# Moving GpSimd's mask work, the first token blocks and w_out's column sums in a fused window attention and feed-forward kernel

## The chip, the cores and the metric

The kernel runs on one core of a Trainium2 chip. The metric is the device time of one execution in microseconds (us); lower is better. TensorE (PE) multiplies matrices, VectorE (DVE) and ScalarE (ACT) work element by element, GpSimd (POOL) does the same and makes masks, and SyncE (SP) issues every DMA here. Each engine runs its own queue in order; semaphores tie the queues together.

## The reference

q, k and v have 8 sequences, 8 heads, 576 tokens and 64 channels. Each token attends to the 32 tokens on either side of it; the heads are then laid side by side and go through a feed-forward layer.

```python
scores = 1/sqrt(64) * q @ k.T                    # per head
mask = abs(pos[:, None] - pos[None, :]) <= 32
attn = softmax(where(mask, scores, -1e9))
x = (attn @ v)                                   # 4608 tokens x 512
h = x @ w_in                                     # 512 x 2048
g = s * relu(h)**2 + b
out = g @ w_out                                  # 2048 x 512
```

All inputs and the output are float32.

## The kernel before

The kernel multiplies in bfloat16, so q, k, v, w_in and w_out are loaded as float32 and cast on the chip. `b` is not added to g: since every g gets the same b, the kernel adds b times the column sums of w_out to the output. These sums, times b, are the tile CVEC.

Nothing in the program is in an order written by hand. Every piece of work is given to `_Graph.add` with an engine (stream), reads, writes, a key and an estimated cost. `plan` simulates the engines with these costs and picks, at each moment, the job that can start first, the key breaking ties; `emit` then writes the queues with the semaphore waits. A key is thus a wish and not a place, and a changed size or an estimated latency (`HELD`, which delays in the plan what uses a piece of w_out) moves other work in the queues. What shares a buffer keeps the order of the calls to `add`.

The stages that matter here, all in the first 70 us:

- **Sequence 0** (`load_pair`, `turn_pair`, `pair_scores`, `first_units`). q and k are loaded by pairs of heads, cast (L687), transposed on TensorE (L700), copied out of PSUM (L705, L706), and multiplied to scores (L939) whose mask is already in PSUM: `opened` adds the tile NEG (L957). GpSimd makes IDENT and NEG first of all (`band`, two selects each, L482 and L487). The five units of `first_units` multiply by v (L864), normalise (L888, L890), and are transposed (L897) and copied to XT (L905).
- **Weights** (`load_weights`). Eight pieces of w_in and eight of w_out, 512 KB each, go through a ring of eight staging tiles STG; GpSimd casts all sixteen (L553). Every load is queued on SP, the w_out loads each waiting for a staging tile.
- **Three early blocks** (`s1`, `early`). The first 512 tokens are split in blocks of 96, 256 and 160 tokens, `sizes`. `s1` multiplies a block by 128-column slices of w_in into one of two PSUM banks W (L1119), 4 or 2 slices to a bank by the block's size (`group`); ScalarE takes the relu into one of three tiles R1 (L1126), and VectorE squares it into GT (L1128). The list `FIRST` gives the order of calls, (block, quarter of w_in), with TURN where the next pair of heads of sequence 1 is put in between, since its transposes use the same banks W. `early` multiplies GT by w_out into four accumulators of 128 tokens each, two in O and two in AVN (L1168); VectorE scales them and adds CVEC (L1153).
- **Masks** (`masks`). From sequence 1 on scores are masked after the exponential by the tiles MASKS. GpSimd makes them after `first_units`: four selects, three copies (L517), four small memsets (L520).
- **Column sums** (`colsum`). TensorE sums w_out's columns into bank SC (L1182, 64 small matmuls), VectorE copies the four parts into a block diagonal of a spare output tile (L1186), one float32 matmul spreads them over the partitions (L1189), and VectorE multiplies by b (L1191). GpSimd clears the two spare tiles first (L1180, L1181).
- **Sequence 1** is turned as sequence 0 was, k cast by VectorE and q by GpSimd (L687). Its scores use SC.
- **Later sequences** are transposed by DMA, and the main loop alternates w_in (L1119) and w_out (L1137) for blocks of 256 and 512 tokens.

Of the kernel before, what the change touches and what calls it, by code (L numbers as in the profile page):

```python
# [9 lines left out]
ALU = mybir.AluOpType  # L10
# [9 lines left out]
NUNIT = (NTILE + 1) // 2  # L20
# [12 lines left out]
TURN = (None, 0)  # L33
FIRST = ((0, 0), (1, 0), (0, 1), (1, 1), (2, 0), (2, 1), (0, 2), (1, 2), (2, 2), TURN, (0, 3), TURN, (1, 3), TURN, (2, 3), TURN)
WOUTE = (("pool", "pool"),) * 4
TAIL = ("act", "dve")
HOST = (("k", 3), ("q", 0))
HELD = (2200.0, 1500.0, 1000.0, 1000.0)
OPEN = -24.4
# [287 lines left out]
def bass_sliding_window_symmetric__then__act_starrelu_kernel(  # L327
# [12 lines left out]

    sizes = [96, 256, 160, 256, 256]
    NE = 3
# [8 lines left out]
    with ExitStack() as es:  # L351
# [18 lines left out]

        NSTG, NNAT, NEX, NXN, NR1, NOUT, XR = 8, 6, 5, 5, 3, 5, 2048
        WIN_BF = sb((128, 4, DFF), BF16, "win")
# [16 lines left out]
        MASK = MASKS[0]  # L389
# [32 lines left out]
        add = g.add  # L422
# [71 lines left out]
        for p0 in (0, 64):  # L494
            band(NEG[p0:p0 + 64, :], NEG[p0:p0 + 64, :], ("NEG", p0), 0, 64, -97, -FAR, source=("NEG", p0))
        ones = ONESW.rearrange("p (one c) -> p one c", one=1).to_broadcast((128, 4, 128))
        add("pe", [lambda e: e.matmul(W[:, 1, :].rearrange("p (a c) -> p a c", a=4), lhsT=ONESW[:, :], rhs=ones,
# [86 lines left out]
        def cast_v(c, u, key, eng, slack):  # L584
            vs, vb, n = number(c, u) % NUNIT, number(c, u) % (2 * NUNIT), 64 * len(tiles(c, u))
            add(eng, (lambda e: e.copy(VB[0:n, vb, :, 0:D], VST[0:n, vs, :, :])) if eng == "act" else
                (lambda e: e.tensor_copy(VB[0:n, vb, :, 0:D], VST[0:n, vs, :, :])),  # L587
                {"act": 617.0, "dve": 420.0, "pool": 750.0}[eng],
                reads=[("VST", vs)], writes=[("V", vb, y) for y in (0, 1)], key=key, slack=slack)

        def load_rows(y, load_key):
# [427 lines left out]
        def attention():  # L1019
            seq = {"k": -200.0}  # L1020

            def nxt():
                seq["k"] += 1.0
                return seq["k"]
# [31 lines left out]
            for step in ORDER1:  # L1056
# [119 lines left out]
        def colsum():  # L1176

            even, block = OUTS[NOUT - 2][:, 0:128], OUTS[NOUT - 1][:, :]
            made = [land["av", 0, NUNIT - 1]]
            add("pool", lambda e: e.memset(even, 1.0 / 32), 150, writes=[("OUTS", NOUT - 2)], key=-19.0, waits=made)  # L1180
            add("pool", lambda e: e.memset(block, 0.0), 500, writes=[("OUTS", NOUT - 1)], key=-19.0, waits=made)  # L1181
            add("pe", [lambda e, fc=fc, x=x: e.matmul(  # L1182
                SC[32 * x:32 * x + 32, 0, 0:128], lhsT=ONESW[:, 0:32], rhs=WOUT_BF[:, fc, 128 * x:128 * x + 128],
                start=(fc == 0), stop=(fc == 15)) for fc in range(16) for x in range(4)],
                1100, reads=["ONESW"] + [("Wout", i, x) for i in range(4) for x in (0, 1)], writes=[("SC", 0)], key=-12.0)
            add("dve", [lambda e, x=x: e.tensor_copy(block[32 * x:32 * x + 32, 128 * x:128 * x + 128],  # L1186
                                                     SC[32 * x:32 * x + 32, 0, 0:128]) for x in range(4)],
                800, reads=[("SC", 0)], writes=[("OUTS", NOUT - 1)], key=-12.0)
            add("pe", lambda e: e.matmul(SC[:, 1, :], lhsT=even, rhs=block, start=True, stop=True),  # L1189
                950, reads=[("OUTS", NOUT - 2), ("OUTS", NOUT - 1)], writes=[("SC", 1)], key=-12.0)  # L1190
            add("dve", lambda e: e.tensor_scalar(CVEC[:, :], SC[:, 1, :], SB128[:, 1:2], None, ALU.mult),  # L1191
                680, reads=[("SC", 1), ("SB128", 1)], writes=[("CVEC", x) for x in (0, 1)], key=P2[0])

# [280 lines left out]
```

## Time and profile before

| | us |
|---|---|
| median of 3 runs | 316.41 |
| lowest and highest run | 315.55, 317.66 |
| the profiled execution, its whole time | 318.05 |
| the profiled execution, its span in the profile | 316.3 |

| engine | busy us | share of the span |
|---|---|---|
| PE | 303.9 | 96% |
| DVE | 194.8 | 62% |
| ACT | 141.9 | 45% |
| POOL | 91.7 | 29% |

The profile is of one execution. A line of a timeline gives start and length in us, engine, source line, operation, what it writes and reads, the tile's size, how many instructions are merged (x8), and in brackets the idle time of the engine before it and what ended that. PE's lengths contain some 0.17 us in which a matmul drains while the next runs, so the time of a group is read from its start to the next group's start. The granted clock is the share of TensorE's full clock.

### The profile page before, as it was taken

The page shows a single profiled execution, that of the slowest core. Times are in us where ns is not written, and L with a number is a line of the kernel's source. Part 1 is how long each engine was busy: PE and PEld are TensorE (multiplying, and loading weights), DVE is VectorE, ACT ScalarE, POOL GpSimd, SP SyncE. Part 2 cuts the span into 40 slices and gives each one's busy share as a digit, 9 for nine tenths or more (in the row PEclk, how much of TensorE's full clock was granted, in tenths as well). Part 3 has the DMA queues.
Part 4 walks back from the last instruction along what each step waited for, and adds up shares of the span by engine and source line. Part 5 has one row for each costly group of instructions (what it writes and reads, how often), then busy time and mean ns, then how long its engine had stood idle before and what let it go on. Part 6 is the DMA issues. An engine that isn't in the chain of part 4 may idle for free.

```text
span 316.3 us, 7961 instructions
## 1 busy us (share of the span) xinstructions
PE 303.9 (96%) x3348; PEld 161.6 (51%) x3348; DVE 194.8 (62%) x387; ACT 141.9 (45%) x224; POOL 91.7 (29%) x110
## 2 busy tenths in 40 slices
PE   6888969999999999999999999999999999999995
PEld 2466656567664454544444444444444444444444
DVE  4666465895897897795577576967445543333312
ACT  4746326356544775654265435444444333333300
POOL 3468973670406136131513411451000000000000
PEclk9799979999999999999999999999999999999999
DMA  6999999998994998799799799996221110000022
GB/s 214 330 380 388 360 229 241 225 188 296 248 182 137 297 166 164 242 206 153 184 290 151 149 251 313 167 169 157 64 63 51 52 46 33 35 35 33 36 96 74
DMA packets 100055, 56.10 MB, mean 177 GB/s; under 512 B 72048, under 2 KB 91248, under 8 KB 100016
## 3 DMA queue, kind: packets, MB, share of 16 engines
q1 hardware_dynamic: 100016, 55.56, 73.0%
q8 instruction: 27, 0.44, 0.6%
q14 instruction: 12, 0.10, 0.1%
HBM read 36.70 MB, written 9.44 MB: 146 GB/s over the span
## 4 chain that ended last, share of the span: by engine, by line
PE 83%; DMA 5%; POOL 4%; SPq 3%; DVE 3%; issue 1%; POOLq 0%
PE w L1119 36%; PE o L1137 35%; PE avn L864 4%; DMA stg<-in_moe_w_in_dram 4%; POOL wout L553 3%; PE sc L806 2%; DMA stg<-in_v_dram 1%; PE avn L1168 1%; SPq L662 1%; PE o L1168 1%; DVE outs L1153 1%; PE w L700 1%; PE avn L897 1%; SPq L673 1%; DVE vb L587 1%
## 5 line engine op out<-in xcount | busy, mean ns | idle before, releaser
L1119 PE MATMUL w<-xt,win 128*128 128x512 bf16 (+3 forms) x768 | 144.8, 327 | 1.1 <-issue 0.6
L1126 ACT ACTIVATE r<-w 128x512 bf16<-128x512 f32 (+2 forms) x148 | 86.6, 586 | 104.0 <-PE w L1119 87.6
L1137 PE MATMUL o<-wout,gt 128*128 128x512 bf16 (+1 forms) x528 | 126.8, 373 | 0.3 <-DVE gt L1128 0.3
L1128 DVE TENSOR_TENSOR gt<-r 128x512 bf16<-128x512 bf16 (+2 forms) x148 | 77.2, 526 | 75.9 <-ACT r L1126 75.5
L1119 PEld LDWEIGHTS w<-xt,win 128*128 128x128 bf16 x768 | 67.7, 98 | 53.9 <-issue 0.8
L1137 PEld LDWEIGHTS o<-wout,gt 128*128 128x128 bf16 x528 | 50.7, 98 | 55.8 <-DVE gt L1128 0.6
L755 POOL CAST nat<-stg 128x1024 bf16<-128x1024 f32 (+1 forms) x21 | 26.6, 1265 | 64.4 <-DMA stg<-in_q_dram 42.5
L772 POOL COPY kt<-ktr 128x512 bf16<-128x512 bf16 (+1 forms) x30 | 31.1, 1037 | 37.4 <-DMA ktr<-nat 35.9
L834 ACT ACTIVATE ex<-sc 128x1024 bf16<-128x1024 f32 (+1 forms) x28 | 28.6, 1023 | 22.5 <-PE avn L864 21.7
L1153 DVE SCALAR_TENSOR_TENSOR outs<-o,sb,cvec 128x512 f32<-128x512 f32 (+1 forms) x35 | 25.4, 728 | 11.4 <-PE o L1137 11.3
L890 DVE TENSOR_TENSOR xn<-avn,rec 128x512 bf16<-128x512 f32 (+1 forms) x31 | 21.3, 688 | 1.0 <-DVE rec L888 0.2
L838 DVE TENSOR_TENSOR ex<-ex,mask 128x1024 bf16<-128x1024 bf16 (+1 forms) x28 | 21.2, 757 | 1.1 <-ACT ex L834 0.5
L864 PE MATMUL avn<-vb,ex 64*64 64x65 bf16 x944 | 19.9, 197 | 0.3
L864 PEld LDWEIGHTS avn<-vb,ex 64*64 64x64 bf16 x944 | 12.9, 106 | 13.2 <-issue 7.8
L755 DVE CAST nat<-stg 128x1024 bf16<-128x1024 f32 (+1 forms) x15 | 12.2, 810 | 3.7 <-DMA stg<-in_k_dram 1.9
L587 DVE CAST vb<-vst 128x512 bf16<-128x512 f32 (+1 forms) x28 | 13.8, 494 | 0.8 <-DMA vst<-in_v_dram 0.7
L888 DVE RECIPROCAL rec<-avn 128x8 f32<-128x8 f32 (+1 forms) x31 | 6.2, 201 | 8.3 <-PE avn L864 8.0
L806 PE MATMUL sc<-qt,kt 64*64 64x128 bf16 x432 | 11.3, 216 | 0.0
L700 PE MATMUL w<-ident,nat 128*128 128x128 bf16 x64 | 7.0, 253 | 3.9 <-POOL nat L687 3.4
L905 ACT COPY xt<-avn 128x512 bf16<-128x512 bf16 (+2 forms) x14 | 7.1, 516 | 6.3 <-PE avn L897 6.3
L705 ACT COPY qt<-w 128x512 bf16<-128x512 bf16 x8 | 4.7, 584 | 11.3 <-PE w L700 11.3
L553 POOL CAST win<-stg 128x1024 bf16<-128x1024 f32 x8 | 8.6, 1080 | 3.6 <-DMA stg<-in_moe_w_in_dram 3.4
(119 smaller groups left out, 156.8 us busy)
## 6 DMA issues: line engine op xcount, KB each, us to landing
out_dram<-outs SPq DMA_DIRECT2D x35, 256.0 KB, 2.6
vst<-in_v_dram SPq DMA_DIRECT2D x28, 256.0 KB, 4.4
stg<-in_k_dram SPq DMA_DIRECT2D x6, 1024.0 KB, 10.6
stg<-in_q_dram SPq DMA_DIRECT2D x6, 1024.0 KB, 6.4
stg<-in_moe_w_in_dram SPq DMA_DIRECT2D x8, 512.0 KB, 9.3
stg<-in_moe_w_out_dram SPq DMA_DIRECT2D x8, 512.0 KB, 10.3
stg<-in_q_dram SPq DMA_DIRECT2D x8, 256.0 KB, 5.3
stg<-in_k_dram SPq DMA_DIRECT2D x8, 256.0 KB, 5.1
```

Source lines behind the costliest of these rows:

```text
L553: add(eng, (lambda e: e.copy(dst, stg)) if eng == "act" else (lambda e: e.tensor_copy(dst, stg)), {"act": 1040.0, "dve": 690.0, "pool": 11 ...
L755: add(eng, lambda e, x=x: e.tensor_copy(nat[0:top, 1024 * x:1024 * x + 1024].rearrange("p (i h d) -> p h i d", h=H, i=2), stg[0:top, :].re ...
L772: add("pool", lambda e, c=c, w=w: e.tensor_copy(KT[slot][:, :, c:c + w].rearrange("p a (s i) -> p a s i", i=4), KTR[slot][:, :, :, c // 4: ...
L834: add("act", lambda e, dst=flat_dst, src=flat_src: e.activation(dst, src, AF.Exp, bias=0.0, scale=0.125), 190 + 0.833 * 512 * len(hs), rea ...
L838: add("dve", lambda e, flat=flat, mask=mask: e.tensor_tensor(flat, flat, mask, ALU.mult), 130 + 0.53 * 512 * len(hs), reads=[("E", ei, hp, ...
L864: return [lambda e: e.matmul(av[64 * x:64 * x + 64, h, 0:D + 1], lhsT=buf[64 * g:64 * g + 64, h % 2, h // 2, c:c + 64], rhs=VB[64 * g:64 * ...
L890: add("dve", lambda e: e.tensor_tensor(XN[xi][0:p1, :].rearrange("p (a c) -> p a c", a=H), av[0:p1, :, 0:D], REC[ri][0:p1, :].rearrange("p ...
L1119: add("pe", [lambda e, g=g, kc=kc: e.matmul(wt[:, g, :], lhsT=WIN_BF[:, kc, (f0 + g) * 128:(f0 + g + 1) * 128], rhs=XT[:, kc, t0 % XR:t0 % ...
L1126: add("act", lambda e: e.activation(rt, wt, AF.Relu, bias=0.0, scale=1.0), 190 + 0.833 * ng * nt, reads=[("W", wb)], writes=[("R1", rb)], ...
L1128: add("dve", lambda e: e.tensor_tensor(GT[gs][:, f0:f0 + ng, g0:g0 + nt], rt, rt, ALU.mult), 130 + 0.53 * ng * nt, reads=[("R1", rb)], wri ...
L1137: add("pe", [lambda e, fc=fc: e.matmul(O[:, ob, 0:cn], lhsT=GT[gs][:, fc, g0:g0 + 128], rhs=WOUT_BF[:, fc, c0:c0 + cn], start=(fc == 0), s ...
L1153: add("dve", lambda e: e.scalar_tensor_tensor(OUTS[us][:, 0:cn], bank, SB128[:, 0:1], CVEC[:, c0:c0 + cn], ALU.mult, ALU.add), 200 + 1.07 ...
```

## The change

GpSimd makes the base mask and clears the two spare tiles right after NEG, ahead of its first cast; the copies and cuts of the mask wait for the last v cast of sequence 1. The first three blocks are 224, 128 and 160 tokens. FIRST has another order of blocks and turns, two entries of HELD go from 1000 to 1500, R1 has four tiles instead of three, and the column sums use bank 1 of AVN, which is also the fourth accumulator of `early`, instead of SC.

```diff
-FIRST = ((0, 0), (1, 0), (0, 1), (1, 1), (2, 0), (2, 1), (0, 2), (1, 2), (2, 2), TURN, (0, 3), TURN, (1, 3), TURN, (2, 3), TURN)
+FIRST = ((0, 0), (0, 1), (1, 0), (1, 1), (2, 0), (0, 2), (2, 1), (1, 2), (2, 2), (0, 3), TURN, TURN, (1, 3), TURN, (2, 3), TURN)
-HELD = (2200.0, 1500.0, 1000.0, 1000.0)
+HELD = (2200.0, 1500.0, 1500.0, 1500.0)
-    sizes = [96, 256, 160, 256, 256]
+    sizes = [224, 128, 160, 256, 256]
-        NSTG, NNAT, NEX, NXN, NR1, NOUT, XR = 8, 6, 5, 5, 3, 5, 2048
+        NSTG, NNAT, NEX, NXN, NR1, NOUT, XR = 8, 6, 5, 5, 4, 5, 2048
...
+        for p0 in (0, 64):
+            band(MASK[p0:p0 + 64, :], ONESW[p0:p0 + 64, :], ("MASK", 0, p0), 0, 64, -96)
+        even, block = OUTS[NOUT - 2][:, 0:128], OUTS[NOUT - 1][:, :]
+        done = [g.tasks[-1]]
+        add("pool", lambda e: e.memset(even, 1.0 / 32), 150, writes=[("OUTS", NOUT - 2)], key=-95.0, waits=done)
+        add("pool", lambda e: e.memset(block, 0.0), 500, writes=[("OUTS", NOUT - 1)], key=-95.0, waits=done)
...
         def masks(after):
-            for p0 in (0, 64):
-                band(MASK[p0:p0 + 64, :], ONESW[p0:p0 + 64, :], ("MASK", 0, p0), 0, 64, -24.0, waits=[after])
             for i, cuts in ((1, ((0, 96), (64, 0))), (2, ((64, 96),)), (3, ((0, 0),))):
                 add("pool", lambda e, i=i: e.tensor_copy(MASKS[i][:, :], MASK[:, :]), 250,
-                    reads=[("MASK", 0, 0), ("MASK", 0, 64)], writes=[("MASK", i, 0), ("MASK", i, 64)], key=0.0)
+                    reads=[("MASK", 0, 0), ("MASK", 0, 64)], writes=[("MASK", i, 0), ("MASK", i, 64)], key=0.0, waits=[after])
...
-            masks(land["av", 0, NUNIT - 1])
...
+            masks(land["vb", 1])
...
         def colsum():
-            made = [land["av", 0, NUNIT - 1]]
-            add("pool", lambda e: e.memset(even, 1.0 / 32), 150, writes=[("OUTS", NOUT - 2)], key=-19.0, waits=made)
-            add("pool", lambda e: e.memset(block, 0.0), 500, writes=[("OUTS", NOUT - 1)], key=-19.0, waits=made)
             add("pe", [lambda e, fc=fc, x=x: e.matmul(
-                SC[32 * x:32 * x + 32, 0, 0:128], lhsT=ONESW[:, 0:32], ...
+                AVN[32 * x:32 * x + 32, 1, 0:128], lhsT=ONESW[:, 0:32], ...
...
-            add("pe", lambda e: e.matmul(SC[:, 1, :], lhsT=even, rhs=block, start=True, stop=True),
+            add("pe", lambda e: e.matmul(AVN[:, 1, :], lhsT=even, rhs=block, start=True, stop=True),
...
-            add("dve", lambda e: e.tensor_scalar(CVEC[:, :], SC[:, 1, :], SB128[:, 1:2], None, ALU.mult),
+            add("dve", lambda e: e.tensor_scalar(CVEC[:, :], AVN[:, 1, :], SB128[:, 1:2], None, ALU.mult),
```

TensorE's queue in the new program, from the first w_out matmul to the fourth accumulator's first (columns x count; "k0" are the transposes of k of pair 0, "acc3" is the third accumulator): acc1 x2, w_in 224 x8, acc2 x2, 160 x8, acc3 x2, 160 x8, acc1 x2, 128 x16, 160 x8, acc2 x2, acc3 x2, 160 x8, 224 x8, acc1 x2, 224 x8, acc2 x2, k0 x4, column sums x64, q0 x4, acc3 x2, k1 x4, acc1 and acc2 x4, q1 x4, L1189, 128 x16, transposes x4, scores of pair 0, acc4 x4. VectorE's queue in the same place: k0's cast, a square, k1's cast, k0's copy out of PSUM, a square, the four copies of the column sums.

More of the change, by code (lines that the diff above doesn't have):

```diff
@@ L589, in cast_v @@
                 reads=[("VST", vs)], writes=[("V", vb, y) for y in (0, 1)], key=key, slack=slack)
+            land["vb", c] = g.tasks[-1]
         def load_rows(y, load_key):
@@ L1176, in colsum @@
         def colsum():
-            even, block = OUTS[NOUT - 2][:, 0:128], OUTS[NOUT - 1][:, :]
-            made = [land["av", 0, NUNIT - 1]]
-            add("pool", lambda e: e.memset(even, 1.0 / 32), 150, writes=[("OUTS", NOUT - 2)], key=-19.0, waits=made)
-            add("pool", lambda e: e.memset(block, 0.0), 500, writes=[("OUTS", NOUT - 1)], key=-19.0, waits=made)
             add("pe", [lambda e, fc=fc, x=x: e.matmul(
-                SC[32 * x:32 * x + 32, 0, 0:128], lhsT=ONESW[:, 0:32], rhs=WOUT_BF[:, fc, 128 * x:128 * x + 128],
+                AVN[32 * x:32 * x + 32, 1, 0:128], lhsT=ONESW[:, 0:32], rhs=WOUT_BF[:, fc, 128 * x:128 * x + 128],
                 start=(fc == 0), stop=(fc == 15)) for fc in range(16) for x in range(4)],
-                1100, reads=["ONESW"] + [("Wout", i, x) for i in range(4) for x in (0, 1)], writes=[("SC", 0)], key=-12.0)
+                1100, reads=["ONESW"] + [("Wout", i, x) for i in range(4) for x in (0, 1)], writes=[("AVN", 1)], key=-12.0)
             add("dve", [lambda e, x=x: e.tensor_copy(block[32 * x:32 * x + 32, 128 * x:128 * x + 128],
[L1187 to L1192, printed above, removed]
+                                                     AVN[32 * x:32 * x + 32, 1, 0:128]) for x in range(4)],
+                800, reads=[("AVN", 1)], writes=[("OUTS", NOUT - 1)], key=-12.0)
+            add("pe", lambda e: e.matmul(AVN[:, 1, :], lhsT=even, rhs=block, start=True, stop=True),
+                950, reads=[("OUTS", NOUT - 2), ("OUTS", NOUT - 1)], writes=[("AVN", 1)], key=-12.0)
+            add("dve", lambda e: e.tensor_scalar(CVEC[:, :], AVN[:, 1, :], SB128[:, 1:2], None, ALU.mult),
+                680, reads=[("AVN", 1), ("SB128", 1)], writes=[("CVEC", x) for x in (0, 1)], key=P2[0])
         units, made = attention(), 0
```

## The prediction

> **What bounds the kernel now.** I read the page first (busy shares, then the 40 slices), next the busy time by stretches, then TensorE's own timeline where it was not full.
>
> ```profile
> PE 303.9 (96%) x3348; PEld 161.6 (51%) x3348; DVE 194.8 (62%) x387; ACT 141.9 (45%) x224; POOL 91.7 (29%) x110
> ```
> ```profile
> 40.00:50.00 10.00, 8.01 (x121) 6.21 (x122) 6.97 (x13) 2.54 (x5) 6.67 (x13) 0.83 1.07 228
> 50.00:60.00 10.00, 10.00 (x136) 5.69 (x133) 6.58 (x12) 6.85 (x11) 3.80 (x6) 1.00 1.18 261
> ```
>
> The columns are the stretch, its length, busy PE, PEld, DVE, ACT, POOL, granted clock, DMA share and GB/s. TensorE is the bound and is full from 50 us on; what can be won lies earlier, above all at 40 us, where both busy time and clock dip. TensorE's timeline (start, length, group, idle before it):
>
> ```profile
> 30.98 0.61 PE L1168 MATMUL o<-wout,gt 128*128 128x512 bf16 x2 [0.74 <-POOL wout L553]
> ...
> 32.41 1.72 PE L1119 MATMUL w<-xt,win 128*128 128x96 bf16 x24
> 33.97 0.59 PE L1168 MATMUL avn<-wout,gt 128*128 128x512 bf16 x2
> ...
> 36.69 0.72 PE L1119 MATMUL w<-xt,win 128*128 128x160 bf16 x8
> 37.24 0.59 PE L1168 MATMUL o<-wout,gt 128*128 128x512 bf16 x2
> 37.67 1.03 PE L1168 MATMUL avn<-wout,gt 128*128 128x512 bf16 x4
> ...
> 41.99 0.99 PE L700 MATMUL w<-ident,nat 128*128 128x128 bf16 x8 [2.42 <-POOL nat L687]
> 42.90 1.90 PE L1182 MATMUL sc<-wout,onesw 128*32 128x128 bf16 x64
> ...
> 46.85 1.04 PE L1119 MATMUL w<-xt,win 128*128 128x256 bf16 x8
> 47.73 0.39 PE L700 MATMUL w<-ident,nat 128*128 128x128 bf16 x4
> 47.95 1.08 PE L1189 MATMUL sc<-outs 128*128 128x512 f32 x2
> ```
>
> TensorE runs dry at 39.57 (41.99 - 2.42) and stands 2.42 us until the first transposes of sequence 1, which wait for GpSimd's cast of q. The stall costs a second time: the clock is granted in stretches of 3.41 us (one at half speed begins at 7.94, one at 42.07), and each follows a poorly filled one:
>
> ```profile
> 4.53:7.94 3.41, 1.97 (x30) 1.02 (x29) 1.34 (x3) 1.69 (x3) 0.61 (x1) 1.00 0.97 294
> 7.94:11.36 3.42, 3.04 (x29) 1.70 (x30) 2.05 (x4) 1.20 (x3) 1.23 (x2) 0.50 1.09 367
> 28.42:31.83 3.41, 2.54 (x30) 1.91 (x29) 2.40 (x5) 1.76 (x4) 3.14 (x5) 1.00 1.05 383
> 31.83:35.24 3.41, 3.41 (x41) 2.77 (x39) 1.13 (x3) 1.52 (x3) 3.16 (x5) 1.00 1.05 386
> 38.66:42.07 3.41, 0.99 (x7) 0.28 (x5) 1.25 (x1) 0.00 (x0) 3.13 (x5) 1.00 0.80 244
> 42.07:45.49 3.42, 3.42 (x81) 3.03 (x82) 1.95 (x5) 0.70 (x2) 2.30 (x6) 0.50 0.97 230
> ```
>
> Stretches 58% (1.97 of 3.41) and 29% busy were followed by half clock, one 74% busy was not. So the stall loses 2.42 us, and half of 3.42, 1.71 us, after it.
>
> **What the stall waits for.** GpSimd's timeline, and two DMA issues asked for one at a time (the last piece of w_out, and k of pair 0 of sequence 1):
>
> ```profile
> 2.79 0.29 POOL L482 TENSOR_SCALAR_AFFINE_SELECT neg<-neg 64x128 bf16<-64x128 bf16 x1
> 3.22 0.29 POOL L487 TENSOR_SCALAR_AFFINE_SELECT neg<-neg 64x128 bf16<-64x128 bf16 x1
> 6.76 0.61 POOL L687 CAST nat<-stg 128x512 bf16<-128x512 f32 x1 [3.25 <-DMA stg<-in_q_dram]
> ...
> 28.13 1.26 POOL L553 CAST win<-stg 128x1024 bf16<-128x1024 f32 x1 [0.32 <-DMA stg<-in_moe_w_in_dram]
> ...
> 33.93 0.52 POOL L1181 MEMSET outs<- 128x512 f32 x1
> ...
> 40.14 1.04 POOL L553 CAST wout<-stg 128x1024 bf16<-128x1024 f32 x1
> 41.24 0.68 POOL L687 CAST nat<-stg 128x512 bf16<-128x512 f32 x1
> ...
> 50.68 1.44 POOL L587 CAST vb<-vst 128x512 bf16<-128x512 f32 x2 [0.77 <-DMA vst<-in_v_dram]
> 55.13 1.04 POOL L755 CAST nat<-stg 128x1024 bf16<-128x1024 f32 x1 [3.01 <-DMA stg<-in_k_dram]
> ```
> ```profile
> L550 SPq DMA_DIRECT2D stg<-in_moe_w_out_dram x1: 367/367/367, 29.4 to 29.4; - x1
> ...
> DMA to landing us min/median/max: 9.4/9.4/9.4
> ```
> ```profile
> L662 SPq DMA_DIRECT2D stg<-in_k_dram x1: 368/368/368, 32.4 to 32.4; - x1
> ...
> DMA to landing us min/median/max: 7.8/7.8/7.8
> ```
>
> From 29.39 (28.13 + 1.26) GpSimd never waits; its last w_out cast ends at 41.18. Between casts stand mask selects, copies and memsets. But w_out's last piece lands only at 38.8 (29.4 + 9.4), the eight pieces 1.36 us apart (524 kB each at the 386 GB/s of the stretch from 31.83), so the first about 29.3; k of sequence 1 lands at 40.2 (32.4 + 7.8).
>
> **The change, part by part.**
>
> *Masks and memsets ahead of the first cast.* Eight casts of 1.04 us with 0.065 between them (40.14 + 1.04 to 41.24) would end at 29.39 + 8.84 = 38.2. The data do not allow it: the last piece lands at 38.8, so the last cast ends at 38.85 + 1.04 = 39.9, 1.3 us earlier and not 3. The first ends near 30.5 instead of 30.93, since no select precedes it, so w_out's first matmuls move up by up to 0.44.
> Ahead of the first cast GpSimd now has four more selects of 0.43 from start to start (2.79 to 3.22) and memsets of 128 and 512 elements, at the cast's rate (1.04 for 1024) 0.65 with two gaps 0.78: 3.51 + 1.72 + 0.78 = 6.0, and the cast waits for its DMA until 6.76: cover 0.75, cost 0. Without that cover, every 0.1 us over delays three q casts by 0.1. The select that TensorE's -FAR matmuls need moves one select back, 0.43; a TensorE wait in that stage, for the cast that starts at 6.76, takes it up.
> The seven mask copies and cuts now follow the last v cast (ends at 50.68 + 1.44 = 52.1): about 1.8 us (estimate: seven small jobs of half a select to a select), to 54, before the cast at 55.13, which waited 3.01 us. Cost 0; if k landed early, at most 1.8 on a cast that does not set the end.
>
> *The restart.* In the new order TensorE's first transposes after its dry point are k's, so VectorE's cast decides, not GpSimd's q cast.
>
> ```profile
> 34.80 1.04 DVE L1128 TENSOR_TENSOR gt<-r 128x512 bf16<-128x512 bf16 x1 [0.62 <-ACT r L1126]
> ...
> 40.21 1.25 DVE L687 CAST nat<-stg 128x512 bf16<-128x512 f32 x1 [1.76 <-DMA stg<-in_k_dram]
> 43.01 0.69 DVE L706 COPY kt<-w 128x512 bf16<-128x512 bf16 x1 [1.55 <-PE w L700]
> ...
> 44.85 1.19 DVE L1186 COPY outs<-sc 32x128 f32<-32x128 f32 x4 [0.51 <-PE sc L1182]
> 46.07 0.44 DVE L687 CAST nat<-stg 128x512 bf16<-128x512 f32 x1
> ...
> 49.09 0.74 DVE L1191 TENSOR_SCALAR cvec<-sc,sb 128x512 f32<-128x512 f32 x1
> ```
>
> The same cast took 1.25 us while GpSimd was casting and 0.44 when it was not. From 40.21 that gives a restart between 40.7 and 41.5. GpSimd's q cast now runs at about 40.0 to 40.6, over half of that: I take 41.05, 0.94 earlier than 41.99 (0.47 to 1.28).
>
> *Blocks, turns, HELD.* Blocks of 224, 128, 160 have the columns of 96, 256, 160 (512) and as many matmuls: total work 0. What moves is the share ahead of the dry point. Before, 16 matmuls each of 96, 256 and 160 columns came after it. Eight of 256 take 0.88 (46.85 to 47.73), eight of 160 take 0.55 (36.69 to 37.24), 16 of 96 take 1.56 - 0.88 = 0.68 (32.41 to 33.97): 3.54 us. Now 16 of 128 (0.055 each, from 47.73 to 47.95) and 16 of 160 come after: 1.98. So 1.56 us of w_in work moves ahead; of w_out's matmuls 16 instead of 20 stand there, four fewer, 0.86 (two take 0.43, 37.24 to 37.67). Net 0.7 us less is left after the restart (0.4 to 0.7). TensorE would run dry near 39.6, as before (its start is up to 0.44 earlier, 0.2 of the moved work falls into the 0.74 idle before 30.98), and stand about 1.4 us.
>
> *The clock.* 1.4 us idle is 59% busy if one stretch holds all of it, next to the 58% that lost the clock; cut by an edge, it lies nearer the 74% that kept it. I count half of 1.71: 0.85 (0 to 1.71).
>
> *Four relu tiles.* They remove ScalarE's waits for VectorE's squares; from 24 to 44 us these are (total, times, longest):
>
> ```profile
> ACT r L1126 <- DVE gt L1128: 0.4, 1, 0.4
> ```
>
> ScalarE is 45% busy; worth 0 (to 0.3).
>
> *Column sums in the fourth accumulator.* SC is freed for the scores, but the fourth accumulator's 16 matmuls must all follow L1189 and the CVEC product. Between the column sums and L1189 TensorE now has 12 transposes (0.66) and six w_out matmuls (1.30): 1.95 us. VectorE must do the k cast of pair 1, one kt copy (0.69), a square and the four copies (1.19) first. With k's transposes and the sums (half of 1.90 at full clock) done near 42.2 TensorE asks at 44.1, and the copies end near 44.4: a wait of 0.3 (0 to 1.2). Behind it stand w_in, transposes and pair 0's scores, for which ScalarE's exp waits. The CVEC product (0.74) then hides behind 16 matmuls of 128, four transposes and the scores.
>
> Sum: -0.94 - 0.7 - 0.85 + 0.3 = -2.2. SP's order is the same through this stage: no DMA term. The profiled execution took 318.05 (span 316.3, 1.75 around it) and would take 315.9; it stood 1.64 above the median of the runs, 316.41, from which the same step gives 314.2. Best of each bound: -1.28 - 0.7 - 1.71 = -3.7, 312.7.
>
> **The rivals.**
> 1. *The clock is kept as well:* an edge of the 3.41 us stretches cuts the remaining idle time, so that none is as empty as 58%: -0.94 - 0.7 - 1.71 + 0.3 = -3.05, 313.4, and 312.7 with the other bounds. For it: 1.4 us is shorter than the 2.42 that lost the clock. Against it: all 1.4 in one stretch leaves 59%, next to the losing row. The Trainium skill, TensorE: Matmul & The Clock Gate, Part 1, also would keep the clock here, since there half speed returns after about 3.4 us of idling; the trace disagrees with that figure, since 2.42 us of idling was enough.
> 2. *The stall only moves:* restart at 41.5, half clock kept, 0.7 at L1189: -0.47 - 0.7 + 0.7 = -0.5, 315.9. For it: the DMA times, which the change does not touch.
> 3. *Slower: the fourth accumulator.* TensorE's queue is in order, and VectorE reaches the four copies behind k0's cast, a square, k1's cast, a kt copy and a second square. At the longest prices above, 41.46 + 1.04 + 1.25 + 0.69 + 1.04 + 1.19 = 46.7. TensorE, restarted at 41.5, asks at 44.6; 2.1 us idle brings a second half clock, 1.71. With the first kept: +2.1 + 1.71 - 0.47 - 0.7 = +2.6, 319.0. It decides once the copies end over 1.4 us after TensorE asks. Against it: GpSimd has gaps there, and one square, not both, need be late.
>
> **How the numbers follow.** Forecast 0.43 (own range 313.0 to 315.6), rival 1 0.30, rival 2 0.17, rival 3 0.10. A measurement can tell about 1%, 3.2 us. Faster by over 1% (under 313.25): over half of rival 1, since the runs scatter by 0.9 below their median (315.55), and a quarter of the forecast, 0.29; slower by over 1% (above 319.57): a part of rival 3 and what I have not seen, 0.08; within: 0.63. Range 311.8 to 317.4: rival 1's best less that 0.9, up to the middle between rivals 2 and 3.
>
> **What would show it.** Right: GpSimd casting only from 29.4, waiting about 0.3 us for DMA before each w_out cast, the last ending near 39.9; TensorE idle 1.0 to 1.8 us instead of 2.42, ended by VectorE's k cast at 40.7 to 41.5; at most one half-clock stretch there; L1189 entered by a wait for VectorE under 0.7; the w_in work of 256 columns earlier by about the sum. Wrong: w_out landing earlier than before, a wait over 1.2 at L1189 or at the fourth accumulator's first matmul, q casts later than 6.8, or a new idle time after 60 us.

## The result, and the profile after

| | before | changed |
|---|---|---|
| median, 22 runs each | 317.49 us (315.3 to 319.2) | 315.37 us (314.14 to 317.37) |
| ratio of times | | 0.9939, 95% interval 0.9921 to 0.9957 |
| profiled execution, its span | 318.05, 316.3 | 317.31, 315.5 |

The change makes the kernel 0.6% faster, some 1.9 us of 317: less than the 1% a measurement of this kernel was taken to tell, though the interval leaves 1 out. In a later set of runs it was 0.9948 (0.9923 to 0.9974). The profiled execution after is one of the slowest of its 22 runs (314.14 to 317.37).

First the page's busy shares of the changed kernel and the engines' shares of the chain that ended last; the third line is that chain of the kernel before.

```profile
PE 296.7 (94%) x3304; PEld 160.6 (51%) x3348; DVE 195.5 (62%) x387; ACT 141.9 (45%) x224; POOL 93.0 (29%) x110
```
```profile
PE 68%; DMA 19%; DVE 6%; issue 3%; SPq 2%; POOL 1%; ACT 0%; POOLq 0%
```
```profile
PE 83%; DMA 5%; POOL 4%; SPq 3%; DVE 3%; issue 1%; POOLq 0%
```

TensorE's records are 44 short of 3348, so its 296.7 us are too few by some and only idle times well above 0.2 us are read. What is to be seen is the chain: GpSimd's 4% is down to 1%, as wanted, and DMA's share went from 5% to 19%. Two stretches follow; those of before stand at the top of the prediction, and the columns are the same (stretch, length, busy PE, PEld, DVE, ACT, POOL, clock, DMA share, GB/s):

```profile
40.00:50.00 10.00, 9.34 (x162) 6.36 (x164) 7.48 (x17) 3.73 (x7) 4.85 (x7) 1.00 1.02 232
...
42.07:45.49 3.42, 3.21 (x23) 1.65 (x23) 3.32 (x10) 1.11 (x2) 1.55 (x3) 1.00 0.97 201
```

The 10 us from 40 on hold 9.34 us of busy TensorE instead of 8.01, and the clock is whole. TensorE's timeline there, and at the three places that matter later:

```profile
38.48 0.59 PE L1173 MATMUL o<-wout,gt 128*128 128x512 bf16 x2
40.24 0.40 PE L705 MATMUL w<-ident,nat 128*128 128x128 bf16 x4 [1.16 <-DVE nat L692]
40.57 1.08 PE L1183 MATMUL avn<-wout,onesw 128*32 128x128 bf16 x64
...
43.33 0.39 PE L705 MATMUL w<-ident,nat 128*128 128x128 bf16 x4
43.87 1.12 PE L1190 MATMUL avn<-outs 128*128 128x512 f32 x2
...
61.94 1.26 PE L1124 MATMUL w<-xt,win 128*128 128x256 bf16 x10
...
88.77 0.32 PE L869 MATMUL avn<-vb,ex 64*64 64x65 bf16 x16 [1.27 <-issue]
...
119.42 0.40 PE L902 MATMUL avn<-ident,xn 128*128 128x128 bf16 x4 [1.30 <-DVE xn L895]
```

The stall is 1.16 us instead of 2.42, ended by VectorE's cast of k, and the column sums take 1.08 instead of 1.90. The cast:

```profile
39.64 0.55 DVE L692 CAST nat<-stg 128x512 bf16<-128x512 f32 x1 [1.59 <-DMA stg<-in_k_dram]
```

The first w_in group of 256 columns starts at 61.94; before:

```profile
65.39 0.83 PE L1119 MATMUL w<-xt,win 128*128 128x256 bf16 x6
```

So 3.45 us are won by there (some 0.6 of it because this execution's transfers landed 0.6 to 0.7 earlier from w_in on). Yet the spans differ by 0.8. The rest went into the two idle times at the end of the list, 1.27 and 1.30 us, at places where the kernel before had none. VectorE shows why; after, then before:

```profile
86.53 0.69 DVE L760 CAST nat<-stg 128x1024 bf16<-128x1024 f32 x1 [1.85 <-DMA stg<-in_k_dram]
87.14 1.52 DVE L843 TENSOR_TENSOR ex<-ex,mask 128x1024 bf16<-128x1024 bf16 x1
```
```profile
85.13 1.53 DVE L755 CAST nat<-stg 128x1024 bf16<-128x1024 f32 x1
86.75 1.08 DVE L1128 TENSOR_TENSOR gt<-r 128x512 bf16<-128x512 bf16 x1
```

VectorE stands 1.85 us at its half of the cast of sequence 3's k; behind it in its queue is the mask multiplication (1.52 us here, while GpSimd casts), and for that TensorE's next AV waits. Before, the same cast had its data. k was asked for at 75.04, 0.6 later than before, and came 11.5 us after; before, 10.3 (the first view asks for k's issue alone, the second also covers q's at 74.0, so k's 10.3 is its longest):

```profile
L752 SPq DMA_DIRECT2D stg<-in_k_dram x1: 890/890/890, 75.0 to 75.0; - x1
...
DMA to landing us min/median/max: 11.5/11.5/11.5
```
```profile
L747 SPq DMA_DIRECT2D stg<-in_k_dram x1: 704/704/704, 74.5 to 74.5; - x1
...
DMA to landing us min/median/max: 6.1/8.2/10.3
```

TensorE came 3.45 us earlier, its data 1.7 later (86.5 against 84.8). The two profiles' stretch from 80 to 120 us, after and before:

```profile
80.00:120.00 40.00, 36.27 (x490) 19.76 (x495) 30.13 (x55) 22.59 (x35) 14.16 (x11) 1.00 1.05 210
```
```profile
80.00:120.00 40.00, 40.00 (x555) 22.26 (x554) 33.71 (x62) 24.19 (x37) 12.69 (x11) 1.00 0.98 203
```

The DMA engines' time is full in both (shares of 1.05 and 0.98); TensorE is full only before. Full means time and not bytes: the same share carried 386 GB/s from 31.83 to 35.24 us in the prediction's rows, and only 203 to 210 here. That gives the theory to test.

### The profile page after: what moved, and what is told of

The parts are those of the page before. It is cut to its first block, busy times and chain, and to the rows that moved or that the text cites. A ratio compares the mean times of both kernels' runs of the same rounds, so it can differ in the third digit from the quotient of the medians.

```text
span 315.5 us, 7901 instructions
## 1 busy us (share of the span) xinstructions
PE 296.7 (94%) x3304; PEld 160.6 (51%) x3348; DVE 195.5 (62%) x387; ACT 141.9 (45%) x224; POOL 93.0 (29%) x110
## 2 busy tenths in 40 slices
DMA packets 100055, 56.10 MB, mean 178 GB/s; under 512 B 72048, under 2 KB 91248, under 8 KB 100016
## 4 chain that ended last, share of the span: by engine, by line
PE 68%; DMA 19%; DVE 6%; issue 3%; SPq 2%; POOL 1%; ACT 0%; POOLq 0%
PE o L1142 30%; PE w L1124 28%; DMA stg<-in_k_dram 10%; DMA stg<-in_moe_w_out_dram 3%; PE avn L869 3%; DMA stg<-in_moe_w_in_dram 3%; DVE gt L1133 2%; PE avn L1173 2%; DMA stg<-in_q_dram 2%; PE sc L811 1%; PE o L1173 1%; DMA vst<-in_v_dram 1%; SPq L667 1%; DVE xn L895 1%; DVE nat L760 1%
## 5 line engine op out<-in xcount | busy, mean ns | idle before, releaser
L1124 PE MATMUL w<-xt,win 128*128 128x512 bf16 (+4 forms) x749 | 140.2, 324 | 3.0 <-ACT r L1131 1.4
L1142 PE MATMUL o<-wout,gt 128*128 128x512 bf16 (+1 forms) x510 | 123.1, 372 | 2.0 <-issue 1.4
L1133 DVE TENSOR_TENSOR gt<-r 128x512 bf16<-128x512 bf16 (+2 forms) x148 | 79.9, 545 | 72.3 <-ACT r L1131 71.9
L760 DVE CAST nat<-stg 128x1024 bf16<-128x1024 f32 (+1 forms) x15 | 11.1, 740 | 7.2 <-DMA stg<-in_k_dram 5.1
L557 POOL CAST wout<-stg 128x1024 bf16<-128x1024 f32 x8 | 9.0, 1122 | 1.7 <-DMA stg<-in_moe_w_out_dram 1.0
L1173 PE MATMUL o<-wout,gt 128*128 128x512 bf16 x29 | 8.2, 379 | 1.0 <-POOL wout L557 0.9
```

The source lines that it names most:

```text
L760: add(eng, lambda e, x=x: e.tensor_copy(nat[0:top, 1024 * x:1024 * x + 1024].rearrange("p (i h d) -> p h i d", h=H, i=2), stg[0:top, :].re ...
L1124: add("pe", [lambda e, g=g, kc=kc: e.matmul(wt[:, g, :], lhsT=WIN_BF[:, kc, (f0 + g) * 128:(f0 + g + 1) * 128], rhs=XT[:, kc, t0 % XR:t0 % ...
L1133: add("dve", lambda e: e.tensor_tensor(GT[gs][:, f0:f0 + ng, g0:g0 + nt], rt, rt, ALU.mult), 130 + 0.53 * ng * nt, reads=[("R1", rb)], wri ...
L1142: add("pe", [lambda e, fc=fc: e.matmul(O[:, ob, 0:cn], lhsT=GT[gs][:, fc, g0:g0 + 128], rhs=WOUT_BF[:, fc, c0:c0 + cn], start=(fc == 0), s ...
L1173: add("pe", [lambda e, fc=fc, bank=bank, gs=gs, g0=g0: e.matmul(bank, lhsT=GT[gs][:, fc, g0:g0 + 128], rhs=WOUT_BF[:, fc, :], start=(fc == ...
```

## The experiments

The first theory, L: the gain is taken back because VectorE's queue stands at its cast until k of sequences 3 and 4 lands. After the first set of runs it became theory D: from 62 to about 220 us the DMA engines are as busy as TensorE, and a TensorE that runs ahead is held wherever it meets a load, by whatever engine. Rivals: the late idle times belong to one execution (S), or to the order of work on the engines and not to transfers (E).

**A second profile of the changed kernel.** No edit.

> The changed kernel once more, unchanged, for a second profile of it. Theory L (the loads take the gain back): what is won by the first 256-column w_in group (61.9 us against 65.4) is partly lost after 80 us, because k of sequences 3 and 4 lands no earlier than before and VectorE's in-order queue stands at its cast; so the profile again shows TensorE idle by 1 us or more between 80 and 120 us, and the ratio to the kernel before stays at 0.992 to 0.996. Rival S (scatter of one execution): the two late idle times of 1.27 and 1.30 us belong to that one execution; here there is none above 0.4 us after 60 us, and the span is near 313.

Measured: 316.8 us median of 12, 0.9948 (0.9923 to 0.9974). Its profiled execution took 315.09 (span 313.3), with all 3348 records:

```profile
100.41 0.34 PE L902 MATMUL avn<-ident,xn 96*128 96x96 bf16 x4 [0.61 <-DVE xn L895]
...
117.24 0.40 PE L902 MATMUL avn<-ident,xn 128*128 128x128 bf16 x4 [0.84 <-DVE xn L895]
```

None of 1 us, none at 87, but 0.61 and 0.84 at 100 and 116 us. So neither S (none above 0.4) nor the sizes of L held: the late idle times came in both executions of the kernel, one at another place and both with other sizes.

**VectorE's share of those casts to GpSimd**, in the changed kernel and in the one before:

```diff
-CASTE = (("pool", "pool"), ("pool", "dve"))
+CASTE = (("pool", "pool"), ("pool", "pool"))
```

> The changed kernel with the one cast of sequences 3 and later that VectorE did (second half of each q, k and rest piece) given to GpSimd as well; TensorE's and SP's orders are untouched. Theory L: VectorE no longer stands behind k's landing, the idle times at 87 and 118 us are gone (each under 0.4 us) and the median is 1.0 to 2.5 us under that of the changed kernel, about 0.988 of the kernel before. Rival S: no change against the changed kernel, 0.994. Rival G: GpSimd's second cast (1.0 us longer) makes the DMA transposes and kt copies late and TensorE waits for those instead: the idle time moves to the first scores of sequences 3 and 4 and the time is the same or worse, 0.994 to 1.000.

> The kernel before with the same casts given to GpSimd, as a control. Theory L: the kernel before is late enough that k has landed when VectorE asks (84.8 against 85.1 us) and it has no idle time above 0.3 us after 60 us, so nothing is gained: within 0.4 us of the kernel before, ratio 0.998 to 1.002. If VectorE's work itself were what is limiting there, it would gain 1 us or more here too.

Measured: changed kernel 317.24 us, 0.9966 (0.9929 to 1.0002); kernel before 317.91, 0.9992 (0.9960 to 1.0023). The control is the null it should be. In the changed kernel the idle time is gone from 87 and 116 us, and the longest one now stands much later, at GpSimd's kt copies, which had waited 5.12 us for k's DMA transpose:

```profile
179.30 0.32 PE L869 MATMUL avn<-vb,ex 64*64 64x65 bf16 x16 [1.32 <-POOL kt L777]
```

That is rival G by its kind of wait, though later than G had it, and no gain against the changed kernel's 0.9948. Theory L falls in this: with the waiting instruction taken off VectorE's queue a wait stands elsewhere. How much of it GpSimd's added casts brought themselves, this run does not separate.

**The stall filled, in the kernel before.** Nine matmuls whose result nobody reads, right ahead of sequence 1's first transposes:

```diff
+add("pe", [lambda e: e.matmul(SC[:, 1, :], lhsT=ONESW[:, :], rhs=WIN_BF[:, 0, 0:512],
+                              start=True, stop=True)] * 9, 1, ..., writes=[("SC", 1)], key=500.0)
...
+g.order.insert(g.order.index(turns[0]), fill)
```

> The kernel before with nine matmuls of 128x512 whose result nobody reads put on TensorE just ahead of the first transposes of sequence 1, that is into the 2.42 us in which it stands (9 x 0.216 = 1.9 us of it). Nothing that waits gets its data earlier, so the restart stays at 42.0. Theory C (a poorly filled stretch of 3.41 us costs the clock of the next): the stretch is 86% busy, half speed does not follow, the column sums take 1.08 instead of 1.90 us, and the first 256-column w_in group comes 1.5 to 1.8 us earlier than 65.4; the median falls by 0.5 to 1.7 us, less than 1.7 where the loads of the later sequences take it back. Rival N (the half speed has another cause): it comes as before, and the time is the same within 0.3 us.

Measured: 317.2 us, 1.0006 (0.9976 to 1.0035). TensorE's timeline, and the two stretches of which, before, the first held 0.99 busy and the second had half clock:

```profile
38.67 2.11 PE L1202 MATMUL sc<-win,onesw 128*128 128x512 bf16 x9
41.26 0.62 PE L700 MATMUL w<-ident,nat 128*128 128x128 bf16 x8 [0.48 <-POOL nat L687]
41.81 1.08 PE L1182 MATMUL sc<-wout,onesw 128*32 128x128 bf16 x64
```
```profile
38.66:42.07 3.41, 2.93 (x38) 1.50 (x40) 1.22 (x2) 0.38 (x1) 2.97 (x8) 1.00 0.91 268
42.07:45.49 3.42, 3.42 (x93) 2.75 (x82) 3.05 (x9) 1.29 (x3) 2.15 (x4) 1.00 1.12 257
```

With the stall filled the clock stays whole in this execution and the sums take 1.08; from the restart to the first 256-column group it is 63.13 - 41.26 = 21.87 us instead of 65.39 - 41.99 = 23.40: 1.53 won, as theory C has it. Nothing of it is seen in the ratio of times; at most 0.8 us by its interval.

**The loads made lighter.** The v loads of sequences 2 and later fetch the same bytes as 2 kB pieces instead of 256-byte rows. These are not the rows that the attention needs, so these kernels leave out a part of v. Every order stays as it was. In the changed kernel, in the kernel before, and in the kernel before with the fill:

```diff
-v[b, :, 64 * j:64 * j + m, :].rearrange("h p d -> p h d")
+v[b].rearrange("h s d -> (h s) d")[0:8 * m, :].rearrange("(p h) d -> p h d", h=8) if c > 1 else ...
```

> The changed kernel with the v loads of sequences 2 and later reading the same bytes as 2 kB pieces that lie together instead of 256-byte rows (the wrong rows of v, so that part of the computation is changed); all orders are the same. Theory D (TensorE, ahead by 3.4 us at 62 us, is held by the DMA stream, which is busy nearly without a break from 26 to 220 us): with a lighter stream no idle time above 0.4 us is left after 60 us, the part from the first 512-column w_in group to the end takes 216.0 to 216.5 us as in the kernel before, and the ratio to the kernel before falls to 0.987 to 0.990 (about 3.4 us of 317). Rival E (the late idle times come from the engines' order, VectorE and GpSimd, not from transfers): they stay, and so does 0.994.

> The kernel before with the same lighter v loads (wrong rows of v from sequence 2 on), as the control of the run above. Theory D: it has no idle time above 0.3 us after 60 us to lose, so its gain is under 0.6 us: 0.998 to 1.001, and the lighter stream is worth 1 us more or better to the changed kernel than to this one. Rival E: also no change; if v traffic slows the kernel before everywhere, both gain alike.

> The kernel before with the nine idle-filling matmuls ahead of sequence 1's first transposes and the lighter v loads (wrong rows of v from sequence 2 on). The fill alone won 1.6 us at the first 256-column group and nothing in the ratio (1.0006). Theory D: with the lighter stream the 1.6 us come through to the end: 0.994 to 0.996. Rival E: still 0.998 to 1.002.

| with lighter v loads | median us | ratio to the kernel before, interval |
|---|---|---|
| kernel before | 317.48 | 0.9968 (0.9943 to 0.9993) |
| before, stall filled | 315.87 | 0.9921 (0.9887 to 0.9954) |
| changed kernel | 314.4 | 0.9879 (0.9842 to 0.9917) |

The same 56.10 MB come in 75,863 packets instead of 100,055. The page's DMA lines with all v rows, and with lighter ones:

```profile
DMA packets 100055, 56.10 MB, mean 178 GB/s; under 512 B 72048, under 2 KB 91248, under 8 KB 100016
```
```profile
DMA packets 75863, 56.10 MB, mean 180 GB/s; under 512 B 44400, under 2 KB 63600, under 8 KB 75824
```

The lighter changed kernel has no idle time above 0.28 us after 60 us any more in its profile, it takes 216.5 us from the first 512-column group to the end (95.80 to 312.3; before, 216.2), and DMA's share of its chain falls from 19% (15% in the second profile) to this:

```profile
PE 84%; DMA 10%; DVE 2%; POOL 1%; SPq 1%; issue 1%; ACT 0%; POOLq 0%
```

By the times alone theory D is not clear of the noise. The fill, worth nothing in the kernel as it is, is worth 1.6 us here (317.48 to 315.87), at the edge of the intervals, and the change 0.9879 / 0.9968 = 0.9911, 2.8 us, where it was worth 1.9: that difference is well inside them. What shows the theory is the part behind the start of the first 256-column group, to the end of the span, in each profile (us):

| | all rows of v as needed | lighter v loads |
|---|---|---|
| kernel before | 250.9 (65.39 to 316.3) | 250.6 (63.28 to 313.9) |
| kernel before, casts to GpSimd | 250.5 (64.50 to 315.0) | |
| kernel before, stall filled | 252.1 (63.13 to 315.2) | 250.5 (63.60 to 314.1) |
| changed kernel | 253.6 (61.94 to 315.5) | 250.8 (61.54 to 312.3) |
| changed kernel, second profile | 252.1 (61.19 to 313.3) | |
| changed kernel, casts to GpSimd | 252.8 (61.63 to 314.4) | |

The work in this part is the same, some 247 us of busy TensorE in each (242.7 in the profile with missing records). With all rows of v as needed, the kernel before takes 250.5 to 250.9 us for it; the filled and the changed kernel, whose TensorE comes there 22.3 to 23.5 us after the start of k's cast instead of 25.2, take 1.2 to 3.1 us more. With lighter loads the difference is gone. So in these executions the transfers take back 1.2 us or more of what was won; what that comes to over all runs stays open. Rival E falls as the cause of it, since every order was kept. Two expectations were off: the kernel before gained 0.3% too, 1 us, where under 0.6 was expected (its interval, 0.9943 to 0.9993, nearly reaches 1), and the filled kernel came to 0.9921 where 0.994 to 0.996 was expected.

**The stores moved behind the loads.** In the changed kernel, the four, three and one stores that stand on SP's queue ahead of the loads of sequences 3, 4 and 5 go right behind them:

```diff
+for t in moved:                      # the stores ahead of these loads
+    g.order.remove(t)
+j = g.order.index(land["loaded", b]) + 1
+g.order[j:j] = moved
```

> The changed kernel with the stores that stand on SP's queue right ahead of the loads of sequences 3, 4 and 5 (four, three and one of 256 KB) moved right behind those loads; nothing else moves. Theory D: k of sequence 3 lands 2 to 3 us earlier (84 instead of 86.5), the late idle times shrink below 0.5 us each and the ratio to the kernel before is 0.988 to 0.992; the stores only come later, where nobody waits. Rival W (what the loads wait for is not the stores ahead but TensorE's and buffers' release): k lands at the same time within 0.7 us and the time stays at 0.994 to 0.995. Rival E: k lands earlier and the idle times stay.

Measured: 316.8 us, 0.9934 (0.9903 to 0.9965), which is the changed kernel's own time and not the 0.988 to 0.992 that theory D expected of it. Its profiled execution took 319.01, well above its median, so only places are read from it. k of sequence 3 lands 9.0 us after its issue instead of 11.5, and the idle times at 87 and 118 us are gone. A new one stands ahead of 145.66 us, behind a wait of VectorE for k:

```profile
145.66 0.32 PE L872 MATMUL avn<-vb,ex 64*64 64x65 bf16 x16 [2.73 <-DVE ex L846]
```
```profile
141.11 0.69 DVE L763 CAST nat<-stg 128x1024 bf16<-128x1024 f32 x1 [2.19 <-DMA stg<-in_k_dram]
```

As far as one execution shows, another order of the same bytes moves the place where TensorE meets a load, as the change of engine did. This was the one candidate for a better version; no run beat the changed kernel's time while it loads all that is needed.

**Part by part.** With the lighter loads, so that nothing is taken back, each part was undone alone. Undoing masks is the old `masks()` and the old memsets, undoing blocks the old `sizes`, `FIRST` and `HELD`:

```diff
-        masks(land["vb", 1])                        # e1: back to land["av", 0, NUNIT - 1], selects and memsets with it
-    sizes = [224, 128, 160, 256, 256]               # e2: [96, 256, 160, 256, 256], with FIRST and HELD as before
-                AVN[32 * x:32 * x + 32, 1, 0:128]   # e3: SC[32 * x:32 * x + 32, 0, 0:128], and what follows from it
-NSTG, NNAT, NEX, NXN, NR1, ... = 8, 6, 5, 5, 4, ... # e4: NR1 = 3
```

> The changed kernel with the lighter v loads (wrong rows of v from sequence 2 on, so that the transfers take nothing back; its median was 314.4), and of the change the masks and memsets put back between GpSimd's w_in and w_out casts; blocks, turns, relu tiles and the sums' bank stay as changed. Theory P (as predicted: without the masks the last w_out cast ends 1.3 us earlier; k's transposes no longer wait for GpSimd, but the column sums right behind them need the last w_out cast): TensorE restarts with k at 40.5 to 41.3 by VectorE's cast, does four transposes, and stands again until the last cast near 41.2: in all 0.6 to 1.3 us lost, 315.0 to 315.7. Rival O (the order of the turns alone did it, and the masks' place is worth nothing): 314.2 to 314.7.

> The changed kernel with the lighter v loads, and of the change the blocks of 96, 256, 160, the old turns and the old held-back values put back; masks, relu tiles and the sums' bank stay as changed. Theory P: GpSimd, free at 39.2, ends q's cast near 40.0, so the restart is at 40.0 to 40.8 and the stall 1.0 to 1.5 us; but less w_in work is left for after it in the changed kernel, worth 0.7 us (0.4 to 0.7): 314.8 to 315.2. Rival B (the blocks and turns make no difference once the masks are moved): 314.2 to 314.6. Rival Q (without them it falls back to the whole of the time before, stall 2.4 us): 316.

> The changed kernel with the lighter v loads, and of the change w_out's column sums put back in the scores' bank. Theory P: the wait for VectorE ahead of the fourth accumulator is worth 0 to 0.3 us either way, since that wait is 0.15 us in the profile of the changed kernel: 314.1 to 314.8, and the first scores of sequence 1 come later by up to 2 us because they need the bank. Rival F (the bank is what opens the way for the scores and so for ScalarE's exp): 315 or more.

> The changed kernel with the lighter v loads and three relu tiles instead of four; TensorE's, GpSimd's and SP's orders are the same. Theory P: worth 0 to 0.3 us, 314.2 to 314.7, so that it also serves as the yardstick for the other three of this set. Rival R: ScalarE's waits for VectorE's squares between 24 and 44 us come through to TensorE: 315 or more.

| undone, with lighter loads | median us | ratio to the kernel before, interval |
|---|---|---|
| nothing (the set of runs above, on another chip) | 314.4 | 0.9879 (0.9842 to 0.9917) |
| masks and memsets | 314.78 | 0.9926 (0.9902 to 0.9951) |
| blocks, turns, HELD | 315.48 | 0.9952 (0.9933 to 0.9970) |
| sums' bank | 314.65 | 0.9923 (0.9894 to 0.9952) |
| fourth relu tile | 314.65 | 0.9919 (0.9890 to 0.9949) |

The last two rows show by how much sets differ: their part behind the first 256-column group takes 250.6 and 250.3 us, as the lighter changed kernel's 250.8, and yet they come to 0.992 where that came to 0.988. By them the change with lighter loads is worth 1.5 us and not 2.8. With the masks or the blocks undone the part takes 251.4 us. Against the yardstick of 314.65, the masks are worth 0.1 us (nearer to rival O than to theory P's 0.6 to 1.3), the blocks and turns 0.8 (P by its sign, a little above its 315.2), the bank and the tile nothing; with the old bank the first scores come 0.4 us later after the restart, not 2. The differences are within the intervals, the blocks' nearest to standing out. TensorE's restart without the moved masks, and without the new blocks and turns:

```profile
40.47 0.40 PE L702 MATMUL w<-ident,nat 128*128 128x128 bf16 x4 [0.36 <-DVE nat L689]
41.36 1.08 PE L1184 MATMUL avn<-wout,onesw 128*32 128x128 bf16 x64 [0.49 <-POOL wout L553]
```
```profile
39.49 0.68 PE L706 MATMUL w<-ident,nat 128*128 128x128 bf16 x8 [1.42 <-POOL nat L693]
```

Each part alone takes most of what both take away (2.42 to some 1.2). With the masks left between the casts, k's transposes need not wait for GpSimd, and the sums behind them wait 0.49 for the last w_out cast: 0.85 us idle in all; later, ahead of 88.66 us, TensorE stood 0.66 us, so the wait there is not wholly gone with lighter loads. With the old turns, q's cast comes early enough because the masks are gone: 1.42. With both it is 1.16 to 1.23. They remove the same wait, so the second adds little. What the old blocks cost in that run does not lie at the stall (its first 256-column group comes 22.12 us after the restart against 21.72 in the lighter changed kernel, but its restart comes 0.3 sooner after the start of k's cast); it lies between 61 and 97 us, where TensorE needs 35.09 us instead of 34.26 from the first 256-column to the first 512-column group, with an idle time of 0.68 for ScalarE's copy of xt.

## Why the prediction was right, and where it was not

*Time and range.* Forecast 314.2 from 316.41, -0.7%; measured -0.61%. The sum of -2.2 stands against -1.94 (0.9939 of 317.49). That they lie so close is luck: by the profiles more is won ahead of 62 us than the sum has, and a part of it is lost behind, which the sum does not have.

*Masks early, cover 0.75 us.* Right in its mechanics. GpSimd's timeline:

```profile
5.33 0.53 POOL L501 MEMSET outs<- 128x512 f32 x1
6.46 0.61 POOL L692 CAST nat<-stg 128x512 bf16<-128x512 f32 x1 [0.60 <-DMA stg<-in_q_dram]
...
28.76 3.78 POOL L557 CAST wout<-stg 128x1024 bf16<-128x1024 f32 x3 [0.18 <-DMA stg<-in_moe_w_out_dram]
33.05 4.83 POOL L557 CAST wout<-stg 128x1024 bf16<-128x1024 f32 x4 [0.51 <-DMA stg<-in_moe_w_out_dram]
38.19 1.04 POOL L557 CAST wout<-stg 128x1024 bf16<-128x1024 f32 x1 [0.31 <-DMA stg<-in_moe_w_out_dram]
...
54.79 0.12 POOL L524 MEMSET mask<- 64x32 bf16 x1
57.45 1.04 POOL L760 CAST nat<-stg 128x1024 bf16<-128x1024 f32 x1 [2.53 <-DMA stg<-in_k_dram]
```

The memsets end at 5.86 (5.33 + 0.53; predicted 6.0), and the first q cast still waits 0.60 for its DMA. The w_out casts wait for DMA, and the last ends at 39.23, 1.1 us after the last piece landed at 38.1 (28.6 + 9.5, below), as predicted (39.9 for a landing at 38.8). The copies end at 54.91 with 2.53 us to spare.

```profile
L554 SPq DMA_DIRECT2D stg<-in_moe_w_out_dram x1: 368/368/368, 28.6 to 28.6; - x1
...
DMA to landing us min/median/max: 9.5/9.5/9.5
```

Once k was turned first the restart no longer hung on them: undone alone they are worth 0.1 us, within the intervals. That the last cast ends 1.3 us sooner was no term of the sum, rightly.

*Restart, -0.94.* Right in mechanism, 0.3 short: VectorE's cast of k ended the stall, 0.55 us long (predicted between 0.44 and 1.25). TensorE restarts 0.60 us after the cast starts (40.24 - 39.64), against 1.78 before (41.99 - 40.21): -1.2, inside 0.47 to 1.28. The idle time is 1.16 where 1.4 was predicted.

*Blocks, -0.7, and L1189, +0.3.* Together -0.4. From the restart to the first 256-column group the changed kernel takes 21.70 us, the kernel before with a whole clock 21.87 (fill): -0.17. With lighter loads it takes 21.72 against 21.87 without the fill and 22.02 with it: -0.15 and -0.30. The wait at L1190 is 0.15 (43.33 + 0.39 to 43.87) and undoing the bank gave nothing, so rival 3's place was never near. So the blocks' term was mis-sized: with the wait of 0.15 taken out it was 0.3 to 0.45 at this place and not 0.7. In the run with the old blocks a further part showed itself after 61 us.

*The clock, -0.85.* In the profile of the kernel before the half-speed stretch cost 1.53 us (23.40 against 21.87 with the stall filled), and 1.59 in that of the kernel before with casts to GpSimd (23.46): the upper part of the range of 0 to 1.71. One such stretch lowers the mean granted clock by 3.41 x 0.5 / 316 = 0.005. Of 85 runs of the kernel before, 20 have 0.998 or more; of 21 runs with the fill, 17; of 34 of the changed kernel, 23. That the fill raises the count this far shows that the stall does cost the clock in many runs. A mean does not say where it was lost, though: in both profiles of the kernel before that lost it behind the stall, a stretch near 8 to 12 us was at half speed too, and the changed kernel with the masks put back had 0.988 from 9.3 to 16.1 us alone. So it is not shown that the changed kernel still loses it at its remaining stall (rival 1); none of its profiles does. If every loss counted were one such stretch, the term would be about 0.7 as a mean over runs (an estimate: 65 of 85 less 11 of 34, times 1.53), so half of 1.71 was a fair booking.

The same stall of 2.42 us was not followed by half speed in the lighter kernel before:

```profile
38.00:41.42 3.42, 1.00 (x6) 0.27 (x4) 1.25 (x1) 0.00 (x0) 3.10 (x6) 1.00 1.01 314
41.42:44.83 3.41, 3.41 (x97) 2.73 (x98) 2.69 (x8) 1.66 (x3) 2.44 (x6) 1.00 1.01 238
```

These two stretches were laid around the stall by choice; where the clock's own edges lay can't be read from an execution that never lost it. An edge in the middle of the stall would leave some 65% busy on either side (an estimate: 1.21 of 3.41 us idle), so the prediction's argument from 58%, 74% and 29% is neither refuted nor proven by it. What it does show is that the length of the stall alone does not decide. The Trainium skill, TensorE: Matmul & The Clock Gate, Part 1, puts the loss after about 3.4 us of idling; this case's profiles show it after 2.42 us in two executions and not in a third.

*What the sum left out.* The step that failed is the one that took 1 us ahead of 62 us for 1 us at the end, with "no DMA term" since SP's order was the same. The order was the same, but the stream was full, and its transfers did not follow a TensorE that came earlier: behind the first 256-column group the changed kernel took 252.1 and 253.6 us where the kernel before took 250.9. Ahead of that group the profiles show -1.2 (restart), -0.2 (blocks and L1190) and -1.5 (clock), -2.9 in all against the sum's -2.2; behind it +1.2 and +2.7, for which nothing was booked. The two errors run against each other. What is left of them, -1.7 and -0.2, is less than the -1.94 of the runs, so how they add up over all runs is not known. The text named the second among the signs ("a new idle time after 60 us") and gave it no price; the row that spoke for it stood in the page of before, DMA's share by slices of 7.9 us, 20 of the first 28 at 0.9 or more:

```profile
DMA  6999999998994998799799799996221110000022
```

*Four relu tiles, 0.* Right: 314.65 without the fourth, and 314.65 with it in the same set of runs (there with the old bank).

Open: whether the kernel before is in truth 0.3% faster with lighter loads, its profile having no idle time to lose, and what sets the scatter of 3 us and more between runs. Some 1.6 us of it lie ahead of the restart: in five profiles whose TensorE has the same work up to there (the changed kernel twice, with casts to GpSimd, with lighter loads, with three relu tiles) it restarts between 39.57 and 41.16 us.

## What to carry to other kernels

Before a gain of an early stage is added to the end of the kernel, look for the next shared stream that is full behind it: if the DMA engines are busy all the time, a microsecond won by the compute engine may be worth no more than its slack at the loads, and here moving the waiting instruction to another engine, or stores in the order, moved the wait. To see it, make the stream lighter in the kernel before and after, with all orders kept, and compare the same part of both profiles from one milestone on: the times of whole runs scatter by more than the effect. And where two edits remove one wait, cost them together: here either of them alone took most of what both took.

## What the runs showed of the hardware beyond that

The clock's loss after the same stall differs between executions: 2.42 us of idling were followed by a half-speed stretch in two profiles and not in a third. At the next milestone such a stretch cost 1.5 to 1.6 us. What it costs at the end is not shown: the 85 runs of the kernel before have medians of 317.24 us (20 runs) at a mean clock of 0.998 or more and 317.85 (65) below, 0.6 us apart, and with lighter loads 316.29 (3 runs) and 317.72 (9).

The same bytes in 24,000 fewer packets, 2 kB for 256 B, came to 0.9968 (0.9943 to 0.9993) in the kernel before, and to 0.9879 against 0.9939 in the changed one (0.992 in the later set), at an unchanged mean rate of 178 to 180 GB/s.

The issue of a store on SP can take long, and what stands behind it in the queue is issued later. Ahead of the loads of sequence 3 the issue of four stores took 3.14 us at 71.25 in the changed kernel's profile and 2.07 at 70.98 in that of the kernel before; behind them a single store took 5.22 us at 82.13 and 0.40 at 84.87. Why, no run here shows.
